# Second-layer products in another order, sums of their weights made later, late gated groups paced by product steps

## The chip, the cores and the metric

The kernel runs on one core of a Trainium2 chip. The metric is the device time of one execution in microseconds (us). Before the change three runs gave 2055.73, 2059.97 and 2067.86 us; the median is 2059.97 us. The profile comes from one further execution of the same program, which took 2061.83 us.

## What is computed

An attention with two parts (downsampled by 4 and put back by repetition, plus a local window of 7 positions) gives x, 2304 tokens of 512 features. A first feed-forward layer with squared relu follows, and then a mixture of eight experts whose gate is balanced over tokens and experts by eight rounds of division:

```python
def _moe2_ref(x, w_gate, w1, w2):
    logits = x @ w_gate                      # 2304 x 8
    P = np.exp(logits - logits.max())
    for _ in range(8):
        P /= P.sum(1, keepdims=True) + 1e-09
        P /= P.sum(0, keepdims=True) + 1e-09
        P *= N / E
    out = np.zeros((N, D), dtype=np.float32)
    for e in range(E):                       # 8 experts
        h = np.maximum(x @ w1[e], 0.0)       # 512 -> 1024
        ye = h @ w2[e]                       # 1024 -> 512
        out += P[:, e:e + 1] * ye
    return out
```

Every expert takes all tokens. The change lies in this mixture, which fills the program from 600 us to the end.

## The kernel before

**Products.** Both layers of an expert are computed as a two-by-two block product with seven block products in place of eight (products 1 to 7). For the second layer a weight block has quarters a[f, d], where f is the parity of the 128-row chunk and d the half of the output columns. Products 1, 2 and 4 take the plain quarters a[0,0], a[1,0] and a[1,1]; products 6, 5, 3 and 7 take sums and differences of quarters (`s2`, `s1`, `s4`, and a[0,0] - a[0,1], which is written over a[0,1]). Each fp32 operand is cut into a high and a low part (`split2`, L462: ScalarE, ACT, writes the high part at L464, VectorE, DVE, or GpSimd, POOL, the difference at L466), and a product of two such operands is three matmuls: high x high, high x low of the input, low of the weight x high.

**First layer.** `l1_second` (L1378) goes through 32 units (8 experts x 4 quarters of the hidden width) times 3 blocks of 768 tokens. `quad` (L1432) combines a unit's products, applies relu and gate on DVE (L1407, L1460), and `store` (L1410) forms sums of the result (L1414, L1416, L1423) and writes them to DRAM as `scr_h`. The first six units finish before the gate rows exist. They are stored without a gate (`scr_c`) and handed to `later` (L1497), which in the middle of the second layer loads such a group back (2 transfers from `scr_c`, 1 of the gate row from `scr_p`), applies the gate with 4 DVE ops (L1520), forms the sums with 4 more (L1525), and writes 6 transfers to `scr_h` (L1528, L1530).

**Second layer.** `l2_second` (L1584) goes through the experts in the order 1 to 7, then 0, and for each through 3 blocks of tokens (`pb`) and the seven products in the order of `PRODUCTS` (L67). One product is 24 matmuls of 128x384 at L1600. Its inputs are two tiles `r` (384 KB each) from `scr_h` (`hidden_loads`, L1564; there are four buffers of this kind), each split by `hidden` (L1577) into a tile named `h`, `i` or `xa`. `collect` (L1614) adds the result to an accumulator; for the first expert it only copies on ACT (L1623), for the others DVE adds (L1627). `l2_weights` (L1540) loads the four quarters of an expert (512 KB each, L1548), makes the four sums (L1556, L1560) and splits all seven weight operands into tiles `w`, `v`, `u`. `finish` (L1631) adds the seven accumulators of a block together (L1638), transposes them on TensorE (PE, L1656) and writes the output.

**What sets the order.** No engine chooses its order on the chip. A planner (class `Order`, L216) runs all these procedures as generators with a cost for each step and writes each engine's instructions in the order that its own clock gives. `("need", f)` holds a procedure back until f is true, `("get", pool)` until a buffer is free, `("wait", event)` until an event fired. Ops that DVE or POOL could do are given to the one that would end first, with `LATE` (3000 ns, L81) in POOL's favour where it is passed (`_w2p`, L369). SyncE (SP) issues every transfer of this part from one in-order queue. `at2["step"]` counts blocks of seven products; the n-th group of `later` is held until that count reaches 1 + 2n.

Of the kernel before, what the change touches and what calls it, by code (L numbers as in the profile page):

```python
# [13 lines left out]
F32R = mybir.dt.float32r  # L14
# [3 lines left out]
ALU = mybir.AluOpType  # L18
# [16 lines left out]
NF2 = DF2 // 128  # L35
# [24 lines left out]
NQ = NF2 // 2  # L60
# [3 lines left out]


OF = {1: (0, 0), 2: (1, 1), 3: (6, 2), 4: (3, 6), 5: (4, 3), 6: (5, 4), 7: (2, 5)}
PRODUCTS = (1, 2, 6, 5, 3, 7, 4)  # L67

BANK = {1: 0, 6: 0, 7: 0, 4: 0, 2: 1, 5: 2, 3: 2}

# [5 lines left out]
NVA, NVD, NQD, NDE, NPT = 1, 2, 2, 2, 2  # L76

AHEAD, WARM, X1FIRST = 3, 4, 3


LATE, SLACK, SLACK_PE = 3000.0, 200.0, 300.0  # L81
# [275 lines left out]
def _dma(nbytes):  # L357
    return ("op", "DMA", nbytes / 360.0)
# [19 lines left out]
def tile_kernel(ctx: ExitStack, tc, qh, kp, vp, qn, kn, vn, vd, bias, mask, w_in, w_out, wg, w12, out):  # L378
# [55 lines left out]
    def get(sl, dt=F32, shape=None, least=1):  # L434
        return ("get", sl, dt, shape, least)
# [734 lines left out]
    PBS = [(0, 0), (1, 0), (0, 1), (0, 2), (1, 1), (1, 2)]  # L1170
    PBS += [(u, pb) for u in range(2, NU - 1) for pb in range(NPB)] + [(NU - 1, 2), (NU - 1, 0), (NU - 1, 1)]
    ev_rows = Event()
    at2 = {"w": 0, "step": -1, "late": 0}
    left_h = {(e, pb): NQ for e in range(E) for pb in range(NPB)}
    s_acc, s_raw, s_h = Many(), Many(), Many()

# [319 lines left out]

    def later(e, pb, q, h):  # L1497

        at2["late"] += 1
        step = min(1 + 2 * at2["late"], 18)  # L1500
        yield ("need", lambda: at2["step"] >= step)
        c = []
        for i in range(3):
            x = yield get(s_p, F32, None, 3 - i)
            c.append(x)
        for i in range(2):
            yield _dma(128 * 2 * TN * 4)
            dma(out=c[i], in_=h[:, 2 * i:2 * i + 2])
        p = c[2]
        a = scr_p[e:e + 1, pb * 2 * TN:(pb + 1) * 2 * TN]  # L1510
        yield _dma(128 * 2 * TN * 4)
        dma(out=p.rearrange("p n t -> p (n t)"),
            in_=bass.AP(tensor=a.tensor, offset=a.offset, ap=[[0, 128], [1, 2 * TN]]))
        t = []
        for i in range(2):
            x = yield get(s_s)
            t.append(x)
        for x, g in ((c[0][:, 0], 0), (c[0][:, 1], 1), (c[1][:, 0], 1), (c[1][:, 1], 0)):
            yield _w2(TN)
            V.scalar_tensor_tensor(out=x, in0=x, scalar=0.0, in1=p[:, g], op0=ALU.max, op1=ALU.mult)  # L1520
        b11, b12, b22, b21 = c[0][:, 0], c[0][:, 1], c[1][:, 0], c[1][:, 1]
        for out, in0, in1, op in ((t[0], b12, b11, ALU.subtract), (t[1], b22, b12, ALU.subtract), (b12, t[1], b11, ALU.add),
                                  (p[:, 0], b21, b12, ALU.subtract)):
            yield _w2(TN)
            V.tensor_tensor(out=out, in0=in0, in1=in1, op=op)  # L1525
        for k, x in ((0, b11), (5, b12), (3, t[0]), (4, t[1]), (6, p[:, 0])):
            yield _dma(128 * TN * 4)
            dma(out=scr_h[e][pb][k, :, q, :], in_=x)  # L1528
        yield _dma(128 * 2 * TN * 4)
        dma(out=scr_h[e][pb][1:3, :, q, :].rearrange("k p t -> p k t"), in_=c[1])  # L1530
        s_p.put(*c)
        s_s.put(*t)
        left_h[e, pb] -= 1
# [5 lines left out]

    def l2_weights():  # L1540
        yield ("need", lambda: at2["w"] == NU)
        for e in EXPERTS:
            a = {}
            for d in range(2):
                for f in range(2):
                    a[f, d] = yield get(s_w)
                    yield _dma(128 * 4096)
                    dma(out=a[f, d], in_=w12[e, f:NF2:2, :, 1, d * 256:(d + 1) * 256].rearrange("q p c -> p q c"))  # L1548
            s1 = yield get(s_w)
            s2 = yield get(s_w)  # L1550
            for k, of in ((1, a[0, 0]), (2, a[1, 0]), (6, s2), (5, s1), (3, None), (7, a[0, 1]), (4, a[1, 1])):
                if k == 1:
                    for out, in0, in1, op in ((s1, a[0, 1], a[1, 1], ALU.add), (a[0, 1], a[0, 0], a[0, 1], ALU.subtract),
                                              (s2, s1, a[0, 0], ALU.subtract)):
                        eng = ENG[(yield _w2p(NQ * 256, LATE))]
                        eng.tensor_tensor(out=out, in0=in0, in1=in1, op=op)  # L1556
                if k == 2:
                    s4 = yield get(s_w)
                    eng = ENG[(yield _w2p(NQ * 256, LATE))]
                    eng.tensor_tensor(out=s4, in0=a[1, 0], in1=s2, op=ALU.subtract)  # L1560
                w2[e, k] = yield from parted(s4 if k == 3 else of, NQ * 256, LATE)
                order.fire(ev_w2[e, k])

    def hidden_loads():  # L1564

# [18 lines left out]
    def l2_second():  # L1584
        for e in EXPERTS:
            for pb in range(NPB):
                at2["step"] += 1
                for k in PRODUCTS:
                    yield ("wait", ev_w2[e, k])
                    w, ps = w2[e, k], []  # L1590
                    for i in range(2):
                        yield ("wait", ev_hk[e, pb, k][i])
                        h = hk.pop((e, pb, k, i))
                        for q in range(2 * i, 2 * i + 2):
                            for d in range(2):
                                if q == 0:
                                    ps.append((yield get(b_q)))
                                yield _pe_r(TN)
                                for m, (a, b) in enumerate(((0, 0), (0, 1), (1, 0))):
                                    PE.matmul(ps[d][:, 0:TN], lhsT=w[a][:, q, d * 128:d * 128 + 128], rhs=h[:, b, q % 2],  # L1600
                                              start=(q == 0 and m == 0), stop=(q == NQ - 1 and m == 2))
                                if q == NQ - 1:
                                    order.add(collect(e, pb, k, d, ps[d]), 1.2)
                        s_h.put(h)
                    if pb == NPB - 1:
                        s_w.put(*w2.pop((e, k)))
                if e == EXPERTS[-1]:
                    order.add(finish(pb), 1.5)
# [22 lines left out]
    def finish(pb):  # L1631

        p = {k: of_acc(pb, k) for k in PRODUCTS}
        yield ("wait", *ev_acc[EXPERTS[-1], pb, 1], *ev_acc[EXPERTS[-1], pb, 2], *ev_acc[EXPERTS[-1], pb, 6])

        def add(out, in0, in1):
            eng = ENG[(yield _w2p(2 * TN))]
            eng.tensor_tensor(out=p[out], in0=p[in0], in1=p[in1], op=ALU.add)  # L1638

        yield from add(2, 1, 2)  # L1640
        yield from add(6, 1, 6)
        yield ("wait", *ev_acc[EXPERTS[-1], pb, 5], *ev_acc[EXPERTS[-1], pb, 3])
        yield from add(1, 6, 5)
        yield from add(3, 1, 3)
        yield ("wait", *ev_acc[EXPERTS[-1], pb, 7], *ev_acc[EXPERTS[-1], pb, 4])
        yield from add(7, 6, 7)
        yield from add(4, 7, 4)
        yield from add(5, 7, 5)
        for nh, (top, low) in enumerate(((2, 4), (3, 5))):
            o = yield get(s_h, F32, [128, 3, 512])  # L1650
            for t in range(3):
# [140 lines left out]
```

## Time and profile before

| | |
|---|---|
| median of three runs | 2059.97 us (2055.73 to 2067.86) |
| the profiled execution | 2061.83 us |
| its span, first to last instruction | 2060.0 us, 30753 instructions |
| mean granted TensorE clock | 0.981 |
| PE busy | 1968.4 us (96%) |
| DVE busy | 1558.6 us (76%) |
| ACT busy | 891.1 us (43%) |
| POOL busy | 671.5 us (33%) |
| transfers | 446.84 MB, mean 217 GB/s |

Busy times are shares of the whole span; stages with different limits are averaged in them. Times within the span are in us from its start. A view of busy time by stages gives for each engine the busy time and in brackets the number of instructions; a timeline gives the start, the length, the engine, the line, what is written and read, and in square brackets how long the engine was idle before and what ended that.

### The profile page before, as it was taken

How to read it: one execution, taken by the hardware profiler on the slowest of the kernel's cores; microseconds unless marked ns; L12 is line 12 of the kernel's file. 1: busy time of each engine (PE TensorE's matmuls, PEld its weight loads, DVE VectorE, ACT ScalarE, POOL GpSimd, SP SyncE). 2: the span in 40 equal slices, each digit the busy share in tenths (PEclk: the TensorE clock that was granted, in tenths of full speed). 3: DMA queues.
4: the chain of work that ended last, by engine and by line, in shares of the span. 5: the costliest groups of instructions: out<-in, count | busy, mean ns of one | idle time of the engine just before them, and what ended most of it. 6: DMA issues, size and time to landing. Idle time of an engine off the chain costs nothing.

```text
span 2060.0 us, 30753 instructions
## 1 busy us (share of the span) xinstructions
PE 1968.4 (96%) x11195; PEld 1854.9 (90%) x11201; DVE 1558.6 (76%) x2140; ACT 891.1 (43%) x1601; POOL 671.5 (33%) x433
## 2 busy tenths in 40 slices
PE   8899998999979999999999999899999989999997
PEld 5577776899979999999999999799999889999997
DVE  6998988681265777777777777667889789988895
ACT  4575546556633222222222222564444344545453
POOL 4445031002004333333333333423424433524451
PEclk8999999999999999999999999899999999999999
DMA  7767686566475666666666667677687768677664
GB/s 200 220 219 226 206 198 196 153 218 210 143 248 194 234 229 212 241 220 228 226 228 235 223 223 264 217 212 236 203 273 233 229 210 283 189 236 229 195 195 143
DMA packets 244848, 446.84 MB, mean 217 GB/s; under 512 B 22440, under 2 KB 144856, under 8 KB 244696
## 3 DMA queue, kind: packets, MB, share of 16 engines
q1 hardware_dynamic: 244696, 444.87, 66.6%
q8 instruction: 88, 1.44, 0.3%
q14 instruction: 64, 0.52, 0.1%
HBM read 280.61 MB, written 164.18 MB: 216 GB/s over the span
## 4 chain that ended last, share of the span: by engine, by line
PE 70%; DVE 14%; DMA 7%; issue 3%; ACT 2%; POOL 1%; SPq 1%; ACTq 0%; DVEq 0%; POOLq 0%
PE b L1374 33%; PE b L1600 23%; PE b L990 6%; PE b L1031 5%; DMA r<-scr_h 3%; DVE xa L466 2%; DMA lk<-in_kp_dram 1%; DVE f L920 1%; DVE f L922 1%; DVE lp L849 1%; DVE z L1525 1%; DVE lp L796 1%; DMA gp<-scr_p 1%; DVE gp L1520 1%; DVE g L1009 1%
## 5 line engine op out<-in xcount | busy, mean ns | idle before, releaser
L1374 PE MATMUL b<-x,w 128*128 128x384 f32 x2688 | 498.0, 338 | 10.3 <-DMA x<-scr_x 4.9
L1374 PEld LDWEIGHTS b<-x,w 128*128 128x128 f32 x2688 | 469.7, 189 | 12.2 <-issue 5.7
L1600 PE MATMUL b<-xa,w 128*128 128x384 f32 x1516 | 342.1, 340 | 13.4 <-DVE xa L466 13.4
L466 DVE TENSOR_TENSOR xa<-r,xa 128x768 fp32r<-128x768 f32 x207 | 285.0, 1387 | 71.1 <-ACT xa L464 68.2
L464 ACT ACTIVATE xa<-r 128x768 fp32r<-128x768 f32 x224 | 189.4, 846 | 238.2 <-DMA r<-scr_h 153.1
L1600 PEld LDWEIGHTS b<-xa,w 128*128 128x128 f32 x1516 | 273.1, 190 | 16.8 <-DVE xa L466 16.7
L1374 PE MATMUL b<-xa,w 128*128 128x384 f32 x1344 | 262.2, 337 | 4.3 <-DMA xa<-scr_x 4.2
L1374 PEld LDWEIGHTS b<-xa,w 128*128 128x128 f32 x1344 | 236.9, 189 | 5.9 <-DMA xa<-scr_x 3.0
L466 POOL TENSOR_TENSOR w<-w,w 128x1024 fp32r<-128x1024 f32 x68 | 151.4, 2227 | 187.1 <-ACT w L464 186.9
L1441 ACT ACTIVATE b<-b 128x384 f32<-128x384 f32 x96 | 45.6, 475 | 326.9 <-PE b L1374 325.3
L1031 PE MATMUL b<-g,s 128*128 128x512 f32 (+1 forms) x756 | 168.9, 369 | 0.9 <-ACT t L1056 0.9
L1447 ACT ACTIVATE q<-b 128x384 f32<-128x384 f32 x192 | 93.3, 490 | 175.6 <-PE b L1374 144.8
L1600 PE MATMUL b<-xa,v 128*128 128x384 f32 x608 | 158.8, 344 | 4.0 <-POOL v L466 2.1
L1228 POOL TENSOR_TENSOR w<-w 128x256 f32<-128x256 f32 x64 | 55.0, 859 | 308.7 <-PE b L1374 257.5
L1031 PEld LDWEIGHTS b<-g,s 128*128 128x128 f32 x756 | 135.9, 188 | 17.9 <-ACT t L1056 1.5
L990 PE MATMUL b<-x,s 128*128 128x512 f32 (+1 forms) x600 | 139.3, 375 | 6.5 <-DVE g L1009 4.8
L1407 DVE SCALAR_TENSOR_TENSOR q<-q,gp 128x768 f32<-128x768 f32 x90 | 127.1, 1412 | 3.1
L990 PEld LDWEIGHTS b<-x,s 128*128 128x128 f32 x600 | 108.0, 191 | 21.8 <-DVE g L1009 6.1
L1471 DVE TENSOR_TENSOR q<-b,q 128x384 f32<-128x384 f32 x96 | 53.5, 557 | 97.8 <-PE b L1374 97.7
L1600 PE MATMUL b<-xa,u 128*128 128x384 f32 x564 | 126.3, 337 | 0.8 <-DVE xa L466 0.6
L1460 DVE SCALAR_TENSOR_TENSOR q<-b,gp 128x384 f32<-128x384 f32 x180 | 100.0, 556 | 34.8 <-PE b L1374 30.7
L1600 PEld LDWEIGHTS b<-xa,v 128*128 128x128 f32 x608 | 113.1, 194 | 5.9 <-POOL v L466 2.4
(250 smaller groups left out, 3337.1 us busy)
## 6 DMA issues: line engine op xcount, KB each, us to landing
r<-scr_h SPq DMA_DIRECT2D x336, 384.0 KB
scr_h<-q SPq DMA_DIRECT2D x90, 576.0 KB
scr_h<-q SPq DMA_DIRECT2D x180, 192.0 KB
scr_h<-q SPq DMA_DIRECT2D x90, 384.0 KB
s<-scr_w SPq DMA_DIRECT2D x85, 256.0 KB
w<-in_w_dram SPq DMA_DIRECT2D x64, 256.0 KB
gp<-scr_p SPq DMA_DIRECT2D x30, 384.0 KB
m<-scr_w SPq DMA_DIRECT2D x43, 256.0 KB
```

Of the source, the lines that this page charges most:

```text
L464: A.activation(out=hi, in_=x, func=AF.Copy)
L466: eng.tensor_tensor(out=lo_, in0=x, in1=hi.bitcast(F32), op=ALU.subtract)
L990: PE.matmul(ps[:, 0:n], lhsT=w[:, a, c], rhs=x[:, b, 0:n], start=(cc == 0 and i == 0), stop=(cc == 3 and i == 2))
L1031: PE.matmul(acc[dc][:, 0:n], lhsT=w[:, a, c], rhs=g[:, b, 0:n], start=(fc == 0 and i == 0), stop=(fc == NF - 1 and i == 2))
L1228: eng.tensor_tensor(out=out, in0=in0, in1=in1, op=op)
L1374: PE.matmul(bank[:, 0:TN], lhsT=w[a][:, iw % 4, cc * 128:cc * 128 + 128], rhs=x[:, b, cc], start=(first and cc == 0 and i == 0), stop=(cc ...
L1407: V.scalar_tensor_tensor(out=x, in0=x, scalar=0.0, in1=p.unsqueeze(1).to_broadcast([128, 2, TN]), op0=ALU.max, op1=ALU.mult)
L1441: A.activation(out=ps[1][:, 0:TN], in_=ps[0][:, 0:TN], func=AF.Copy)
L1447: A.activation(out=c[:, place], in_=ps[bank][:, 0:TN], func=AF.Copy)
L1460: V.scalar_tensor_tensor(out=c[:, i], in0=ps[bank][:, 0:TN], scalar=0.0, in1=p[:, 0], op0=ALU.max, op1=ALU.mult)
L1471: V.tensor_tensor(out=c[:, 2], in0=ps[0][:, 0:TN], in1=c[:, 2], op=ALU.add)
L1600: PE.matmul(ps[d][:, 0:TN], lhsT=w[a][:, q, d * 128:d * 128 + 128], rhs=h[:, b, q % 2], start=(q == 0 and m == 0), stop=(q == NQ - 1 and m ...
```

## The change

Four things are altered. The order of the second layer's products becomes 1, 2, 4, 6, 5, 3, 7, so that the three with plain quarters come first. `l2_weights` splits those three quarters first and makes the sums behind them; for the first expert it passes 0 in place of `LATE`. `at2["step"]` counts products, not blocks; a group of `later` begins at the seventh product, and each of its nine transfers waits for one further product step (`pace`). `finish` adds in an order that fits the new last product.

```diff
-PRODUCTS = (1, 2, 6, 5, 3, 7, 4)
+PRODUCTS = (1, 2, 4, 6, 5, 3, 7)
...
+PACE = 1
...
-    at2 = {"w": 0, "step": -1, "late": 0}
+    at2 = {"w": 0, "step": 0}
...
     def later(e, pb, q, h):
-        at2["late"] += 1
-        step = min(1 + 2 * at2["late"], 18)
-        yield ("need", lambda: at2["step"] >= step)
+        yield ("need", lambda: at2["step"] >= 7)
+
+        def pace():
+            n = at2["step"] + PACE
+            return ("need", lambda: at2["step"] >= n)
+
...
         for i in range(2):
+            yield pace()
             yield _dma(128 * 2 * TN * 4)
             dma(out=c[i], in_=h[:, 2 * i:2 * i + 2])
...
+        yield pace()
         yield _dma(128 * 2 * TN * 4)
...
         for k, x in ((0, b11), (5, b12), (3, t[0]), (4, t[1]), (6, p[:, 0])):
+            yield pace()
             yield _dma(128 * TN * 4)
...
+        yield pace()
         yield _dma(128 * 2 * TN * 4)
...
     def l2_weights():
...
+        late = lambda e: 0.0 if e == EXPERTS[0] else LATE
+
+        def parts(e, k, x):
+            hi = yield get(s_w, F32R)
+            lo_ = yield get(s_w, F32R)
+            yield from split2(x, NQ * 256, hi, lo_, late(e))
+            w2[e, k] = (hi, lo_)
+            order.fire(ev_w2[e, k])
+
         for e in EXPERTS:
             a = {}
-            for d in range(2):
-                for f in range(2):
...
+            for d, f in ((0, 0), (0, 1), (1, 1), (1, 0)):
...
+            for k, of in ((1, a[0, 0]), (2, a[1, 0]), (4, a[1, 1])):
+                yield from parts(e, k, of)
             s1 = yield get(s_w)
             s2 = yield get(s_w)
...
+            for out, in0, in1, op in ((s1, a[0, 1], a[1, 1], ALU.add), (s2, s1, a[0, 0], ALU.subtract)):
+                eng = ENG[(yield _w2p(NQ * 256, late(e)))]
+                eng.tensor_tensor(out=out, in0=in0, in1=in1, op=op)
+            s_w.put(a[1, 1])
+            yield from parts(e, 6, s2)
+            yield from parts(e, 5, s1)
+            s_w.put(s1)
+            for out, in0, in1 in ((s2, a[1, 0], s2), (a[0, 1], a[0, 0], a[0, 1])):
+                eng = ENG[(yield _w2p(NQ * 256, late(e)))]
+                eng.tensor_tensor(out=out, in0=in0, in1=in1, op=ALU.subtract)
+            s_w.put(a[0, 0], a[1, 0])
+            for k, of in ((3, s2), (7, a[0, 1])):
+                yield from parts(e, k, of)
+                s_w.put(of)
...
             for pb in range(NPB):
-                at2["step"] += 1
                 for k in PRODUCTS:
+                    at2["step"] += 1
...
     def finish(pb):
...
+        yield from add(2, 1, 2, 1, 2)
+        yield from add(6, 1, 6, 4, 6)
+        yield from add(4, 6, 4)
+        yield from add(1, 6, 5, 5)
+        yield from add(3, 1, 3, 3)
+        yield from add(5, 1, 7, 7)
+        yield from add(4, 4, 7)
```

What the planner makes of it. Up to the last products of the first layer the instructions are the same in both programs (line numbers move by two). Three places differ in ways that the prediction speaks of.

POOL, from its last op for the first layer on (L466 and L468 with 128x1024 are low parts of weights, L1556, L1560 and L1575 their sums), before:

```order
L466 TENSOR_TENSOR w_1700_12088<-w_1691_12024,w_1699_12087 128x768
L1556 TENSOR_TENSOR w_1720_12277<-w_1717_12251,w_1719_12266 128x1024
L1556 TENSOR_TENSOR w_1717_12251<-w_1705_12126,w_1717_12251 128x1024
L1556 TENSOR_TENSOR v_1722_12299<-w_1720_12277,w_1705_12126 128x1024
L466 TENSOR_TENSOR v_1736_12386<-w_1705_12126,v_1735_12385 128x1024
L1560 TENSOR_TENSOR v_1743_12427<-w_1712_12225,v_1722_12299 128x1024
L466 TENSOR_TENSOR v_1750_12448<-w_1712_12225,v_1749_12447 128x1024
```

and now:

```order
L468 TENSOR_TENSOR w_1700_12088<-w_1691_12024,w_1699_12087 128x768
L468 TENSOR_TENSOR w_1865_13064<-v_1794_12676,w_1829_12846 128x1024
L468 TENSOR_TENSOR v_1872_13105<-w_1801_12695,v_1870_13096 128x1024
L468 TENSOR_TENSOR v_1881_13149<-w_1805_12720,v_1878_13139 128x1024
L1575 TENSOR_TENSOR v_1890_13189<-u_1813_12766,w_1805_12720 128x1024
```

The eleven ops for the first expert are gone from POOL; what now follows is for the second one. They stand on DVE, between the last ops of the first layer (names `q`) and the splits of the second layer's inputs (`h`, `xa`, `i`, read from tiles `r`). DVE there, before:

```order
L1460 SCALAR_TENSOR_TENSOR q_1725_12315<-b_1723_12300,gp_1642_11540 128x384
L1407 SCALAR_TENSOR_TENSOR q_1725_12315<-q_1725_12315,gp_1642_11540 128x768
L466 TENSOR_TENSOR h_1727_12333<-r_1721_12298,h_1727_12333 128x768
L1414 TENSOR_TENSOR q_1737_12405<-q_1725_12315 128x768
L466 TENSOR_TENSOR xa_1732_12369<-r_1728_12334,xa_1732_12369 128x768
L1416 TENSOR_TENSOR q_1737_12405<-q_1737_12405,q_1725_12315 128x384
L1423 TENSOR_TENSOR q_1729_12340<-q_1715_12241,q_1729_12340 128x384
L466 TENSOR_TENSOR xa_1733_12370<-r_1730_12345,xa_1733_12370 128x768
```

and now, up to the low part of the second product's weights (`v_1731`):

```order
L1473 TENSOR_TENSOR q_1725_12315<-b_1723_12300,q_1725_12315 128x384
L468 TENSOR_TENSOR xa_1735_12374<-r_1732_12348,xa_1735_12374 128x768
L1409 SCALAR_TENSOR_TENSOR q_1725_12315<-q_1725_12315,gp_1642_11540 128x768
L1462 SCALAR_TENSOR_TENSOR q_1725_12315<-b_1723_12300,gp_1642_11540 128x384
L1425 TENSOR_TENSOR q_1727_12330<-q_1715_12241,q_1727_12330 128x384
L1416 TENSOR_TENSOR q_1742_12425<-q_1725_12315 128x768
L468 TENSOR_TENSOR xa_1736_12375<-r_1733_12359,xa_1736_12375 128x768
L1418 TENSOR_TENSOR q_1742_12425<-q_1742_12425,q_1725_12315 128x384
L468 TENSOR_TENSOR xa_1740_12412<-r_1737_12387,xa_1740_12412 128x768
L468 TENSOR_TENSOR i_1743_12427<-r_1741_12413,i_1743_12427 128x768
L468 TENSOR_TENSOR h_1745_12437<-r_1744_12428,h_1745_12437 128x768
L468 TENSOR_TENSOR v_1731_12343<-w_1712_12225,v_1730_12342 128x1024
```

The low part of the first product's weights stands ten places ahead of this piece; that of the second stands behind the splits of `r_1737`, `r_1741` and `r_1744`, the fifth to seventh tiles.

SP's queue at the stores of the first late group (`scr_h_0_143`), before:

```order
L1574 DMA r_1944_13489<-scr_h_1_150 128x768
L1528 DMA scr_h_0_143<-gp_1905_13287 128x384 x2
L1528 DMA scr_h_0_143<-z_1913_13315 128x384
L1528 DMA scr_h_0_143<-z_1914_13316 128x384
L1528 DMA scr_h_0_143<-gp_1907_13289 128x384
L1530 DMA scr_h_0_143<-gp_1906_13288 128x2x384
L1574 DMA r_1949_13526<-scr_h_1_150 128x768
```

and now:

```order
L1536 DMA scr_h_0_143<-gp_1796_12689 128x384
L1598 DMA r_1843_12940<-scr_h_2_148 128x768
L1598 DMA r_1848_12966<-scr_h_2_148 128x768
L1536 DMA scr_h_0_143<-gp_1796_12689 128x384
L1598 DMA r_1850_12980<-scr_h_2_148 128x768
L1598 DMA r_1855_13006<-scr_h_2_148 128x768
L1536 DMA scr_h_0_143<-z_1825_12825 128x384
```

Two loads of `r` now stand between any two stores of a group, and the group stands in the first expert.

## Rows read from the trace of the kernel before

**Rows 1.** The page, busy time of each engine (us, share of the span, instructions).

```profile
PE 1968.4 (96%) x11195; PEld 1854.9 (90%) x11201; DVE 1558.6 (76%) x2140; ACT 891.1 (43%) x1601; POOL 671.5 (33%) x433
```

**Rows 2.** Chain of waits in order of time (start, length, what).

```profile
626.58 657.35 PE b L1374 x3786
...
1297.16 3.10 DMA r<-scr_h
...
1303.63 6.23 DMA r<-scr_h
```

**Rows 3.** Busy time by stages: length, PE, PEld, DVE, ACT, POOL, clock, DMA share, GB/s.

```profile
1283.00:1336.00 53.00, 41.30 (x193) 38.95 (x192) 37.67 (x32) 27.97 (x39) 25.32 (x11) 0.81 0.70 229
1336.00:1745.00 409.00, 390.40 (x2184) 383.82 (x2183) 330.24 (x364) 190.24 (x238) 153.65 (x61) 0.98 0.73 235
...
1336.00:1390.00 54.00, 54.00 (x313) 54.00 (x312) 31.78 (x26) 33.94 (x54) 13.30 (x5) 1.00 0.72 215
1390.00:1425.00 35.00, 32.08 (x183) 31.43 (x183) 28.53 (x33) 17.23 (x22) 15.36 (x6) 1.00 0.60 194
...
1465.00:1495.00 30.00, 26.55 (x129) 25.54 (x128) 25.97 (x30) 10.79 (x13) 10.69 (x4) 0.83 0.58 185
1495.00:1530.00 35.00, 33.04 (x187) 32.08 (x187) 28.36 (x33) 17.96 (x22) 13.79 (x6) 1.00 0.73 228
1530.00:1560.00 30.00, 30.00 (x174) 30.00 (x173) 23.58 (x32) 10.71 (x13) 5.23 (x2) 1.00 0.88 306
...
1590.00:1625.00 35.00, 31.30 (x171) 29.25 (x170) 30.36 (x37) 13.62 (x16) 11.72 (x6) 1.00 0.66 214
...
1660.00:1682.00 22.00, 16.80 (x86) 16.16 (x85) 21.89 (x26) 8.68 (x10) 8.12 (x3) 0.92 0.48 134
...
1720.00:1745.00 25.00, 24.29 (x138) 23.59 (x137) 22.66 (x26) 10.17 (x12) 11.53 (x5) 1.00 0.93 316
```

**Rows 4.** PE's timeline: start of the second layer, and 1523 us.

```profile
1290.51 2.29 PE L1374 MATMUL b<-x,w 128*128 128x384 f32 x6 [4.51 <-DVE q L1471]
...
1297.18 3.89 PE L1600 MATMUL b<-h,v 128*128 128x384 f32 x11 [4.06 <-DVE h L466]
...
1522.69 2.01 PE L1600 MATMUL b<-h,w 128*128 128x384 f32 x10 [1.27 <-POOL w L466]
```

**Rows 5.** DVE's and POOL's timeline, 1268 to 1300 us.

```profile
1280.38 0.96 DVE L1407 SCALAR_TENSOR_TENSOR q<-q,gp 128x768 f32<-128x768 f32 x1
...
1286.04 2.67 POOL L1556 TENSOR_TENSOR v<-w,w 128x1024 f32<-128x1024 f32 x1
1286.43 3.10 DVE L1414 TENSOR_TENSOR q<-q 128x768 f32<-128x768 f32 x1
```

**Rows 6.** Instructions of single lines, 1250 to 2060 us (duration min/median/max in ns).

```profile
L466 DVE TENSOR_TENSOR xa<-r,xa x207: 937/958/3171, 1297.9 to 2032.6; 128x768 fp32r<-128x768 f32 x104
...
L464 ACT ACTIVATE xa<-r x224: 827/847/856, 1285.9 to 2031.7; 128x768 fp32r<-128x768 f32 x112
...
L1520 DVE SCALAR_TENSOR_TENSOR gp<-gp,gp x24: 541/551/2685, 1399.2 to 1723.8; 128x384 f32<-128x384 f32 x24
```

**Rows 7.** Timeline within the second late group, 1466 to 1490 us.

```profile
1475.74 2.49 DVE L1520 SCALAR_TENSOR_TENSOR gp<-gp,gp 128x384 f32<-128x384 f32 x1
...
1478.15 3.11 DVE L466 TENSOR_TENSOR xa<-r,xa 128x768 fp32r<-128x768 f32 x1
...
1481.32 4.21 PE L1600 MATMUL b<-xa,w 128*128 128x384 f32 x12 [2.75 <-DVE xa L466]
```

**Rows 8.** Busy time by stages, for the transfers (last two columns).

```profile
1400.00:1750.00 350.00, 331.40 (x1845) 324.82 (x1844) 297.69 (x339) 150.03 (x177) 134.37 (x55) 0.98 0.73 236
1525.00:1550.00 25.00, 25.00 (x146) 25.00 (x145) 21.02 (x29) 10.09 (x13) 5.23 (x2) 1.00 0.90 318
```

**Rows 9.** Timeline of the end.

```profile
2047.27 3.69 DVE L1638 TENSOR_TENSOR q<-q,q 128x768 f32<-128x768 f32 x4
2050.14 4.46 PE L1656 MATMUL b<-ident,q 128*128 128x128 f32 x22 [4.28 <-DVE q L1638]
```

More of the change, by code (lines that the diff above doesn't have):

```diff
@@ L1541, in l2_weights @@
         yield ("need", lambda: at2["w"] == NU)
+        late = lambda e: 0.0 if e == EXPERTS[0] else LATE
[5 more added lines that the diff above has]
+            order.fire(ev_w2[e, k])
         for e in EXPERTS:
             a = {}
-            for d in range(2):
-                for f in range(2):
-                    a[f, d] = yield get(s_w)
-                    yield _dma(128 * 4096)
-                    dma(out=a[f, d], in_=w12[e, f:NF2:2, :, 1, d * 256:(d + 1) * 256].rearrange("q p c -> p q c"))
+            for d, f in ((0, 0), (0, 1), (1, 1), (1, 0)):
+                a[f, d] = yield get(s_w)
+                yield _dma(128 * 4096)
+                dma(out=a[f, d], in_=w12[e, f:NF2:2, :, 1, d * 256:(d + 1) * 256].rearrange("q p c -> p q c"))
+            for k, of in ((1, a[0, 0]), (2, a[1, 0]), (4, a[1, 1])):
+                yield from parts(e, k, of)
@@ L1549, in l2_weights @@
             s1 = yield get(s_w)
             s2 = yield get(s_w)
[L1551 to L1562, printed above, removed]
+            for out, in0, in1, op in ((s1, a[0, 1], a[1, 1], ALU.add), (s2, s1, a[0, 0], ALU.subtract)):
+                eng = ENG[(yield _w2p(NQ * 256, late(e)))]
+                eng.tensor_tensor(out=out, in0=in0, in1=in1, op=op)
@@ L1633, in finish, with add @@
         p = {k: of_acc(pb, k) for k in PRODUCTS}
-        yield ("wait", *ev_acc[EXPERTS[-1], pb, 1], *ev_acc[EXPERTS[-1], pb, 2], *ev_acc[EXPERTS[-1], pb, 6])
-        def add(out, in0, in1):
+        def add(out, in0, in1, *after):
+            for k in after:
+                yield ("wait", *ev_acc[EXPERTS[-1], pb, k])
             eng = ENG[(yield _w2p(2 * TN))]
             eng.tensor_tensor(out=p[out], in0=p[in0], in1=p[in1], op=ALU.add)
[L1640 to L1648, printed above, removed]
+        yield from add(2, 1, 2, 1, 2)
[5 more added lines that the diff above has]
+        yield from add(4, 4, 7)
         for nh, (top, low) in enumerate(((2, 4), (3, 5))):
```

## The prediction

> **What bounds the kernel now.** Begin with the page. TensorE (PE) is busy 96% of the span at a mean clock of 0.98 [rows 1, 3], so only its idle time, and its time at the lower clock, can be won back. The chain of waits gives the full rate: 3786 matmuls in 657.35 us are 0.1736 us each [rows 2], so a second-layer product of 24 takes 4.17 us. Next, busy time by stages, where the losses lie: multiply a stretch's matmuls by 0.1736 and compare with its length. From 1283 to 1336 us the first layer ends and the first seven second-layer products run. The 193 matmuls need 33.5 of 53 us: **19.5 us lost**. From 1336 to 1745 us, 2184 need 379.1 of 409 us: **29.9 us lost** [rows 3]. The change touches both places; 49.4 us is all it can win there.
>
> Why is PE waiting? In the first place, PE's timeline names DVE at the two long gaps [rows 4]. DVE's and POOL's timelines show the cause: a DVE op of 768 columns took 0.96 us at 1280; beside POOL, which makes sums of weights (2.67 us each), the next such op took 3.10 [rows 5]. The usual time is 0.95 [rows 6]. In the second place it is the same pair. The six groups of `later` (8 small DVE ops each) are gated between 1399 and 1724 us [rows 6]. The stretches around them lose 35 - 31.8 = 3.2, 30 - 22.4 = 7.6, 0, 5.3, 7.1 and 1.0 us [rows 3]. The group without loss ran beside next to no POOL work; its ops took 0.55 us. Where POOL splits weights, DVE ops take 2.5 to 3.1 us, PE waits up to 2.75 us [rows 7] and then runs partly at the lower of its two levels, 1.2 GHz (granted clock 0.83 in that stretch) [rows 3].
>
> **Part 1, the first expert's weights.** The order of instructions shows eleven POOL ops (4 sums, 7 low parts) gone to DVE, and nothing left on POOL there. Removed: POOL's 11 ops of some 2.67 us. Added to DVE: 11 ops of 1024 columns. No row shows one on DVE alone; 0.55 us for 384 columns and 0.95 for 768 [rows 6] give 1.2 by the same slope, an estimate, 13.2 us in all. It isn't free: all of it lies ahead of the first seven products.
>
> I follow DVE's order down from 1280.4 us [rows 5], up to where both programs are alike, with these three durations. The low part of product 1's weights is done at 1282.6, the first half of its inputs at 1286.7 (PE waits 0.7 us), the sum on which the last first-layer product waits at 1288.6 (1290.5 before [rows 4]), the second input half at 1288.1. PE does product 1 and that last piece by 1291.9. Then a new wait: product 2's low part `v_1731` stands on DVE behind three splits of tiles whose buffers only come free when the splits ahead of them end, at 1286.7, 1288.1 and 1289.6. A load then needs 3.1 to 6.2 us [rows 2], ACT 0.85 and DVE 0.95 [rows 6], so `v_1731` ends near 1298.2. PE waits 6.3 us; its remaining 22 matmuls of product 2 run, as after the 4.06 us gap [rows 4], at half rate, 0.35 us each, until 1305.9. What stands behind on DVE (two sums 1303, low part of product 6 at 1306) is earlier than PE needs it. Five more products at 4.17 end at 1326.8. Before, the seventh ended at 1336.0 (193 matmuls less 24 of the first layer [rows 3] are seven products): **-9.2 us**. Bounds: loads of 6.2 us and another product at half rate, +5, give -4; no wait at `v_1731` gives -9.2 - 6.3 - 3.8 = -19, all that is lost there.
>
> **Part 2, order of products and sums later.** For later experts products 1, 2, 4 need no sums; POOL's eleven ops per expert are the same. Before, low parts on POOL came late near 1520 us [rows 4], in a stretch that loses 35 - 32.5 = 2.5 us [rows 3]. With three products (12.5 us) ahead of the first sum these waits go: -2.5, counted in part 3's sum. If POOL falls behind instead, product 6 of the second expert is late next. Its high part stands 3.5 products ahead on ACT, 14.6 us, and only a low part of 2.7 us follows it, so I cost that at nothing.
>
> **Part 3, paced groups.** Bytes and ops stay, nine transfers per group, 2.56 MB. They now stand on SP's queue one per product step, two or three loads apart, not in bursts of three and six. A store waiting on its DVE op would hold up the loads behind it; the ops come earlier than the paced stores, so that wait costs nothing. What counts is where the groups meet POOL. By the place of collected products on DVE the groups now lie at products 20, 21 to 24, 33 to 36, 45 to 48, 58 to 62 and 72 to 75 (before 22 to 25, 36, 50, 64, 78, 92). Weights are made around products 18 to 28, 39 to 48, 60 to 69. So the first group lies in the first expert, where DVE is busy 31.78 of 54 us [rows 3], and costs nothing; the third and sixth meet no weights and cost 0.5 us each (0 and 1.0 before); the second, fourth and fifth meet them. Four such groups lost 3.2, 7.6, 5.3 and 7.1, a mean of 5.8; three make 17.4, and the sum is 18.4 against 29.9: **-11.5 us**, weights' waits included. Bounds: all clear, -29.9, or five collisions, 29 us, next to no gain.
>
> **Tail.** The last seven additions run on DVE after the last product, 0.95 us each, and the last transposes wait for them [rows 9]. Before, the first half of the output needed six of them, now all seven: **+0.9 us**.
>
> **Sum.** The profiled execution took 2061.83 us (span 2060.0), 1.86 above the median of the runs. 2061.83 - 9.2 - 11.5 + 0.9 = 2042.0: **2042 us**. Its own range is 2034 to 2051.
>
> **Rivals.**
> A. *Both places come clear*: loads land in 3.1 us, so `v_1731` isn't waited for, and only one group meets POOL. 2061.8 - 18 - 20 + 1 = 2025. For it: the third group before lost nothing. Against: DVE's order puts the splits ahead of `v_1731`. Chance 0.17.
> B. *The pacing only moves the collisions* (or its steps, counted by the planner, don't hold on the chip): the groups lose 28 to 30 us as before and only part 1 counts, 2061.8 - 9.2 + 0.9 = 2053.5; with part 1 at its bad bound, 2058.7. For it: the same eight ops and the same POOL work in the same 400 us. Chance 0.26.
> C. *Slower, transfers become the bound.* From step 8 to 75 a product needs two loads (0.79 MB), 0.10 MB of weights and up to 0.26 MB of a group, 1.15 MB. At full rate that is 276 GB/s; from 1400 to 1750 us the queue moved 236 [rows 8]. Should that be its sustained most, a step takes 4.87 us, 0.70 more, over 67 steps 47 us. With the collisions hidden behind that it gives 47 - 29.9 - 9.2 + 0.9 = +9, with none hidden 18 more; between the two, 2080. It decides once the sustained rate stays under some 242 GB/s. Against it: 318 GB/s over 25 us without a wait of PE [rows 8]. The Trainium skill, DMA: Bandwidth & Descriptors, section "Specifications", puts a core's share of HBM at about 358 GB/s; by it this case would cost nothing, and no run here shows that rate held for long. Chance 0.07.
>
> **Chances and range.** The forecast has 0.50. A measurement can tell about 0.5% from no change, 10.3 us, so faster means below 2051.5 on this scale: forecast and A, with a little of B, **0.69**; same, the rest of B and the forecast's upper edge, **0.23**; slower, C and a part 1 gone wrong, **0.08**. For 8 in 10 the range reaches from A's 2025 to B's 2058.
>
> **What would show it.** Part 1: no POOL op from 1281 to about 1350 us, DVE splits at 0.95 us throughout, one PE gap of some 6 us ahead of the third matmul of product 2, released by a DVE op of 1024 columns, and product 7 done near 1327. Part 3: no burst of three group loads on SP; PE gaps near products 21 to 24, 46 and 60, with DVE ops of 2.5 us beside POOL ops, and none near 34 and 74. PE gaps released by a load of `r` would speak for C, gaps at all six groups for B. The forecast is wrong if the stretch up to product 7 isn't 5 us shorter, or if the stretch behind it still loses over 25 us.

## The result, and the profile after

The changed kernel takes **2043.55 us** (median of four runs, 2043.14 to 2044.38) against 2060.71 us of the kernel before (four runs beside them, 2055.73 to 2067.86). The ratio is 0.9915, with a 95% interval of 0.9885 to 0.9944: faster by 0.85%. The profiled execution took 2043.14 us with a span of 2041.4 us; TensorE's mean granted clock was 0.983.

The page, busy time of each engine after (us, share of the span, instructions), the answer to [rows 1]:

```profile
PE 1964.4 (96%) x11201; PEld 1853.8 (91%) x11201; DVE 1542.9 (76%) x2157; ACT 891.6 (44%) x1601; POOL 626.2 (31%) x416
```

POOL is busy 45 us less and has 17 instructions fewer, DVE has 17 more; yet DVE is busy 16 us less, because its operations are stretched less. PE is busy only 4 us less (time at half clock counts as busy), so most of the gain is idle time.

Busy time by stages after (length, PE, PEld, DVE, ACT, POOL, clock, DMA share, GB/s), the answer to [rows 3]:

```profile
1280.00:1322.00 42.00, 36.27 (x192) 35.67 (x191) 35.63 (x42) 26.03 (x38) 0.00 (x0) 0.92 0.84 288
1322.00:1745.00 423.00, 406.46 (x2293) 401.76 (x2292) 334.36 (x391) 203.27 (x252) 146.22 (x57) 0.99 0.75 238
...
1322.00:1390.00 68.00, 68.00 (x393) 68.00 (x392) 46.51 (x47) 43.17 (x66) 15.69 (x6) 1.00 0.80 254
1390.00:1420.00 30.00, 24.92 (x128) 23.30 (x127) 25.63 (x27) 11.41 (x15) 14.59 (x5) 0.94 0.70 221
1420.00:1485.00 65.00, 65.00 (x375) 65.00 (x374) 54.67 (x69) 31.76 (x37) 21.88 (x9) 1.00 0.82 256
1485.00:1510.00 25.00, 20.83 (x117) 19.87 (x116) 21.28 (x25) 7.69 (x10) 9.12 (x4) 1.00 0.59 182
1510.00:1550.00 40.00, 40.00 (x231) 39.81 (x230) 27.66 (x40) 18.89 (x23) 4.23 (x2) 1.00 0.92 296
1550.00:1580.00 30.00, 25.24 (x134) 24.24 (x133) 27.43 (x29) 10.48 (x12) 14.57 (x6) 0.94 0.44 128
1580.00:1610.00 30.00, 27.48 (x154) 26.54 (x153) 23.17 (x27) 13.63 (x16) 12.81 (x5) 1.00 0.73 249
1610.00:1640.00 30.00, 30.00 (x174) 30.00 (x173) 23.06 (x34) 13.99 (x17) 8.23 (x4) 1.00 0.88 295
1640.00:1745.00 105.00, 105.00 (x603) 105.00 (x602) 84.95 (x100) 52.25 (x61) 45.09 (x18) 1.00 0.71 223
```

With 0.1736 us per matmul again, 1322 to 1745 us loses 423 - 398.1 = **24.9 us**; before, the stretch behind product 7 lost 29.9 [rows 3]. It is lost in four places: 7.8 us from 1390, 4.7 from 1485, 6.7 from 1550 and 3.3 from 1580. The gating operations of the six groups start at 1335, 1381, 1442, 1493, 1551 and 1619 us, so these places are the second, the fourth and the fifth group with what follows it. The four add up to 22.5 us: a matmul on the border of two stretches is counted in both. The first, third and sixth group cost nothing.

The first layer's end and the second layer's start after, timelines of DVE, PE and POOL (start, length, engine, line, what, idle time before it and what ended that), the answer to [rows 4, 5]:

```profile
1285.75 0.95 DVE L1409 SCALAR_TENSOR_TENSOR q<-q,gp 128x768 f32<-128x768 f32 x1
...
1291.30 0.96 DVE L468 TENSOR_TENSOR i<-r,i 128x768 fp32r<-128x768 f32 x1 [0.21 <-ACT i L466]
1292.18 0.95 DVE L468 TENSOR_TENSOR h<-r,h 128x768 fp32r<-128x768 f32 x1
1293.05 1.22 DVE L468 TENSOR_TENSOR v<-w,v 128x1024 fp32r<-128x1024 f32 x1
...
1294.32 8.98 PE L1624 MATMUL b<-xa,v 128*128 128x384 f32 x34 [5.73 <-DVE v L468]
...
1357.75 2.39 POOL L468 TENSOR_TENSOR w<-v,w 128x1024 fp32r<-128x1024 f32 x1 [100.87 <-DVE i L468]
```

POOL does nothing for 100 us. No DVE operation is stretched: 768 columns take 0.95 us, 1024 columns 1.22. The gap of 4.51 us ahead of the first layer's last piece and that of 4.06 us in product 1 [rows 4] are gone. One of 5.73 us stands in product 2 in their place, on the low part that waited behind the input splits; the 34 matmuls behind it take 8.98 us, 3.1 more than at the full rate.

**Where the time went, measured from one operation.** Up to a 768-column gating operation on DVE (L1407 before, L1409 after; two more of its kind follow before the first layer ends) the two programs are the same. It starts at 1273.08 us before and at 1269.86 after: 3.2 of the 18.7 us between the profiled executions lie ahead of anything that the change touches. So the table counts from there, to the end of product 7 (the 168th second-layer matmul; each trace holds all 4032 of them), and from there to the end of the span. Each row is one execution. How much these stretches vary between executions of one kernel was not measured, so differences of a few us rest on a single profile each. "After" is the full change, the others are the experiments below; all are in us.

| kernel | to product 7 | product 7 to end | median of its runs |
|---|---|---|---|
| before | 63.1 | 723.8 | 2060.71 |
| after | 52.2 | 719.3 | 2043.55 |
| weights alone | 50.7 | 726.7 | 2050.79 |
| paced groups alone | 62.2 | 712.4 | 2052.10 |
| old order, weights on DVE | 57.3 | 724.3 | 2057.71 |
| first expert's weights on POOL | 69.3 | 718.3 | 2061.13 |
| groups in POOL-free products | 52.2 | 701.4 | 2025.16 |
| the same in bursts | 51.3 | 699.9 | 2026.44 |
| groups on the weights | 51.1 | 727.3 | 2057.67 |
| product 2's low part first | 52.7 | 716.5 | 2045.02 |
| POOL-free, low part first | 52.5 | 697.0 | 2023.24 |
| the same, tail swapped | 52.8 | 698.2 | 2023.32 |

The full change wins 10.8 us up to product 7 and 4.6 us behind it, 15.4 together; the medians differ by 17.2.

### The profile page after: what moved, and what is told of

The parts are those of the page before. It is cut to its first block, busy times and chain, and to the rows that moved or that the text cites. A ratio compares the mean times of both kernels' runs of the same rounds, so it can differ in the third digit from the quotient of the medians.

```text
span 2041.4 us, 30758 instructions
## 1 busy us (share of the span) xinstructions
PE 1964.4 (96%) x11201; PEld 1853.8 (91%) x11201; DVE 1542.9 (76%) x2157; ACT 891.6 (44%) x1601; POOL 626.2 (31%) x416
## 4 chain that ended last, share of the span: by engine, by line
PE 79%; DVE 9%; DMA 7%; issue 2%; ACT 2%; POOL 1%; SPq 1%; DVEq 0%; ACTq 0%; POOLq 0%
PE b L1376 33%; PE b L1624 31%; PE b L992 6%; PE b L1033 6%; DMA o<-in_w_in_dram 1%; DMA r<-scr_h 1%; DMA lk<-in_kp_dram 1%; DVE f L922 1%; DVE xa L468 1%; DVE f L924 1%; DVE lp L851 1%; DMA x<-scr_x 1%; DMA o<-in_w_out_dram 1%; DMA lk<-in_vp_dram 0%; DMA xa<-scr_x 0%
## 5 line engine op out<-in xcount | busy, mean ns | idle before, releaser
L468 DVE TENSOR_TENSOR xa<-r,xa 128x768 fp32r<-128x768 f32 x210 | 260.3, 1253 | 63.1 <-ACT xa L466 62.4
L466 ACT ACTIVATE xa<-r 128x768 fp32r<-128x768 f32 x224 | 189.5, 846 | 243.5 <-DMA r<-scr_h 136.1
L1624 PE MATMUL b<-xa,w 128*128 128x384 f32 x1232 | 263.4, 337 | 5.4 <-DVE xa L468 5.4
L1376 PE MATMUL b<-xa,w 128*128 128x384 f32 x1344 | 263.7, 339 | 3.0 <-DMA xa<-scr_x 3.0
L1376 PEld LDWEIGHTS b<-xa,w 128*128 128x128 f32 x1344 | 238.5, 190 | 4.6 <-DMA xa<-scr_x 3.7
L1624 PEld LDWEIGHTS b<-xa,w 128*128 128x128 f32 x1232 | 219.6, 189 | 6.8 <-DVE xa L468 6.7
L468 POOL TENSOR_TENSOR w<-w,w 128x1024 fp32r<-128x1024 f32 x71 | 158.6, 2234 | 191.8 <-ACT w L466 191.7
L1624 PE MATMUL b<-xa,u 128*128 128x384 f32 x736 | 186.6, 337 | 3.1 <-DVE xa L468 3.1
L1624 PE MATMUL b<-xa,v 128*128 128x384 f32 x720 | 167.9, 342 | 5.7 <-DVE v L468 5.7
L1624 PEld LDWEIGHTS b<-xa,u 128*128 128x128 f32 x736 | 134.0, 188 | 4.0 <-DVE xa L468 4.0
L1624 PEld LDWEIGHTS b<-xa,v 128*128 128x128 f32 x720 | 131.7, 192 | 6.1 <-DVE v L468 6.1
L1409 DVE SCALAR_TENSOR_TENSOR q<-q,gp 128x768 f32<-128x768 f32 x90 | 125.1, 1390 | 3.1
```

Source lines behind the costliest of these rows:

```text
L466: A.activation(out=hi, in_=x, func=AF.Copy)
L468: eng.tensor_tensor(out=lo_, in0=x, in1=hi.bitcast(F32), op=ALU.subtract)
L1376: PE.matmul(bank[:, 0:TN], lhsT=w[a][:, iw % 4, cc * 128:cc * 128 + 128], rhs=x[:, b, cc], start=(first and cc == 0 and i == 0), stop=(cc ...
L1409: V.scalar_tensor_tensor(out=x, in0=x, scalar=0.0, in1=p.unsqueeze(1).to_broadcast([128, 2, TN]), op0=ALU.max, op1=ALU.mult)
```

## The experiments

The kernel before ran beside every batch; each ratio is to those runs.

### The two halves apart

The full change with the groups of the kernel before:

```diff
-        yield ("need", lambda: at2["step"] >= 7)
...
-            yield pace()
...
+        at2["late"] += 1
+        step = 7 * min(1 + 2 * at2["late"], 18) + 1
+        yield ("need", lambda: at2["step"] >= step)
```

> The change without its paced groups: groups start at the old blocks (products 22, 36, 50, ...) and issue their transfers in bursts. My theory: the transition up to product 7 keeps its whole gain of about 10.8 us, the groups cost what they did before (about 25 us, with only the 2.5 us of weights' waits gone): 2060.7 - 10.8 - 2.5 = about 2047 us, 4 us above the full change. Rival: the early products need the paced groups too, or the weights' new order makes the groups worse; then 2052 us or more.

Measured: 2050.79 us, ratio 0.9945 (0.9924 to 0.9966). That is between my theory (2047) and the rival (2052 or more). The transition keeps its gain (50.7 us), and the rest is no better than before (726.7 against 723.8). The waits on late weights near 1520 us [rows 4] are gone, but the 2.5 us that I had counted for them don't appear: of the 48 small group operations (4 gating, 4 sums in each group) 17 take over 1 us there, 13 before.

The kernel before with the new `later` and the count of products:

```diff
-                at2["step"] += 1
                 for k in PRODUCTS:
+                    at2["step"] += 1
...
-        step = min(1 + 2 * at2["late"], 18)
-        yield ("need", lambda: at2["step"] >= step)
+        yield ("need", lambda: at2["step"] >= 7)
...
+            yield pace()
```

> The kernel before with paced, back-to-back groups only; sums and products of the second layer in their old order, the first expert's on VectorE and GpSimd as before. My theory: the 19.5 us of the transition stay lost, the groups lose some 5 us less than their 29.9: about 2056 us. Rival B of the prediction (pacing only moves the collisions): 2061 us, no change. A third reading, that the gain behind product 7 came from the weights' order and not from the pacing, also gives 2061 here, and then the run with the weights alone gives the full change's 2043.

Measured: 2052.10 us, ratio 0.9942 (0.9923 to 0.9960). The transition is as it was (62.2), and behind product 7 11.4 us are gone. That is more than I expected, and more than the full change wins there (4.6). In these profiles, then, the halves don't add. By the medians that is not clear of noise: the halves win 0.55 and 0.58%, the full change 0.85%, each known to 0.2 or 0.3. It isn't that more of the full change's groups meet POOL: 11 of the 48 operations take over 1 us in the full change, 14 in the run with paced groups alone. But in the full change PE also waits 2.9 us for late weights (shown below), and between product 7 and 1745 us the granted clock falls to its lower level twice (from 1413 and from 1567 us), in the other run never. Why a collision costs more there wasn't tried. Third reading refuted: pacing alone does gain.

### Does the place of a group decide?

The full change, with each group tied to a product number. By its timeline POOL makes weights near products 16 to 27, 37 to 52, 58 to 73 and so on, every 21. A group's DVE operations come some four to seven products behind its start, so one that starts at 8 + 21n has them ahead of that work, and one that starts at 17 + 21n within it:

```diff
-        yield ("need", lambda: at2["step"] >= 7)
+        at2["late"] += 1
+        first = 8 + 21 * at2["late"]
+        yield ("need", lambda: at2["step"] >= first)
```

(`late` starts at -1; the second kernel has 17 in place of 8.)

> The full change, but each group starts at a product in which GpSimd makes no weights: groups start at products 8, 29, 50, 71, 92 and 113 instead of back to back; the pacing of one transfer per product stays. My theory (a group costs where its small VectorE operations meet GpSimd's weight work, 0.5 us elsewhere): of the 24.9 us lost behind product 7 about 18 go, 2043.5 - 18 = about 2026 us. Rival (what is lost there is the transfers, or GpSimd against the splits of inputs with no group in it): within 4 us of 2043.5, whatever the place.

> The full change, but all six groups start four products before a new expert begins (products 17, 38, 59, 80, 101, 122), so that their VectorE operations fall into GpSimd's weight work each time. My theory: six collisions at 5.8 us each, 35 us against the 24.9 lost now: 2043.5 + 10 = about 2053 us. Rival (place doesn't matter): 2043.5 within 3 us.

Measured: 2025.16 us, ratio 0.9817 (0.9790 to 0.9844), and 2057.67 us, ratio 0.9983 (0.9960 to 1.0007). My theory held for the first (2026) and was 5 us low for the second (2053). Same work, same pacing, the same number of transfers: 32.5 us between the two, and only the place of the groups differs. The transfers move with the operations, but no PE gap over 0.3 us behind product 7 is ended by a load in either run. The gating operations' durations point at the operations (minimum, median and maximum in ns, first and last start). After:

```profile
L1527 DVE SCALAR_TENSOR_TENSOR gp<-gp,gp x24: 544/551/2769, 1335.0 to 1624.8; 128x384 f32<-128x384 f32 x24
```

In the POOL-free products, with the busy time by stages:

```profile
L1529 DVE SCALAR_TENSOR_TENSOR gp<-gp,gp x24: 546/550/560, 1340.7 to 1792.5; 128x384 f32<-128x384 f32 x24
...
1324.00:1745.00 421.00, 419.12 (x2395) 417.09 (x2394) 349.08 (x401) 211.81 (x262) 151.83 (x58) 1.00 0.76 239
```

On the weights, with the timelines of DVE and PE:

```profile
L1529 DVE SCALAR_TENSOR_TENSOR gp<-gp,gp x24: 540/548/2605, 1390.9 to 1872.2; 128x384 f32<-128x384 f32 x24
...
1679.29 2.53 DVE L1529 SCALAR_TENSOR_TENSOR gp<-gp,gp 128x384 f32<-128x384 f32 x1
1681.74 3.15 DVE L468 TENSOR_TENSOR i<-r,i 128x768 fp32r<-128x768 f32 x1
...
1699.20 0.44 PE L1626 MATMUL b<-xa,u 128*128 128x384 f32 x1 [2.52 <-DVE xa L468]
```

Away from POOL no gating operation exceeds 0.56 us, and the stretch, which holds five of the six groups, loses 421 - 415.8 = 5.2 us in place of 24.9. POOL is as busy there as in the full change (151.83 us), and it stretches even more of the input splits: from product 8 to product 134, 69 of the 242 on DVE take over 1.3 us, against 52 of 239 in the full change and 30 of 247 in the kernel with its groups on the weights. So stretching alone costs little; it costs where a group's operations stand on DVE beside it. On the weights, operations of 2.5 and splits of 3.15 us make PE wait at every group, at the first one also 4.28 and 1.42 us for late weights.

The POOL-free kernel with its transfers in bursts (`PACE = 0`):

> Groups start at products 8, 29, 50, 71, 92 and 113 as in the run with placed groups, but issue their transfers in bursts as the kernel before does. My theory (place alone decides): within 3 us of 2025. Rival (a burst of 1.2 MB ahead of the input loads makes TensorE wait some 1 us at each of the six groups): 2030 us or more, with TensorE gaps released by loads.

Measured: 2026.44 us, ratio 0.9826 (0.9800 to 0.9852); my theory held, and no PE gap over 0.6 us behind product 7 is ended by a load. The pacing wins nothing that can be measured once the place is right: what it did in the change was to move the groups. Five of the groups here have one operation of 1.5 us beside POOL, at no cost that shows. In bursts some splits of inputs move to POOL and its weights come late instead (PE's timeline):

```profile
1759.95 2.00 PE L1626 MATMUL b<-xa,v 128*128 128x384 f32 x10 [0.80 <-POOL v L468]
1765.52 2.03 PE L1626 MATMUL b<-h,w 128*128 128x384 f32 x10 [1.14 <-POOL w L468]
```

### What wins in the transition?

The full change with the first expert's weights on POOL where it is free:

```diff
-        late = lambda e: 0.0 if e == EXPERTS[0] else LATE
+        late = lambda e: LATE
```

> The full change, but the first expert's sums and low parts go to GpSimd wherever it is free, as the later experts' do; the order of products (1, 2, 4 first) stays. My theory (the gain of the transition is VectorE freed of the work beside it): input splits of some 3 us come back, a gap of 3 to 5 us ahead of the last piece of the first layer, and 7 to 10 us of the gain are lost: about 2052 us. Rival (the gain is the product order, which needs no sums at the start): within 3 us of 2043.5.

Measured: 2061.13 us, ratio 0.9988 (0.9973 to 1.0002): not 2052, the whole gain is gone. Up to product 7 it takes 69.3 us, 6.2 more than the kernel before. Timelines of POOL, DVE and PE:

```profile
1291.59 2.59 POOL L468 TENSOR_TENSOR v<-w,v 128x1024 fp32r<-128x1024 f32 x1 [1.36 <-ACT v L466]
1291.90 3.09 DVE L468 TENSOR_TENSOR h<-r,h 128x768 fp32r<-128x768 f32 x1
...
1295.04 0.69 PE L1624 MATMUL b<-h,w 128*128 128x384 f32 x1 [5.10 <-DVE h L468]
...
1319.06 1.01 PE L1624 MATMUL b<-h,u 128*128 128x384 f32 x2 [7.41 <-ACT u L466]
```

The gap of 5.10 us was expected; that of 7.41 us at product 6, whose sum is now made late and is then split on ACT, was not. Making sums later, with POOL still making them, is a loss here up to product 7.

The kernel before with the first expert's weights on DVE, in the old order:

```diff
+        late = lambda e: 0.0 if e == EXPERTS[0] else LATE
...
-                        eng = ENG[(yield _w2p(NQ * 256, LATE))]
+                        eng = ENG[(yield _w2p(NQ * 256, late(e)))]
...
-                w2[e, k] = yield from parted(s4 if k == 3 else of, NQ * 256, LATE)
+                w2[e, k] = yield from parted(s4 if k == 3 else of, NQ * 256, late(e))
```

> The kernel before (old product order, old groups), with only the first expert's sums and low parts taken from GpSimd to VectorE. Three sums then stand ahead of product 1's low part on VectorE, and that part behind six input splits. My theory (both halves are needed: no op beside VectorE and no sums ahead of the first product): the operations keep 0.95 us but a gap of some 6 to 10 us opens ahead of product 1's low part, and the stretch up to product 7 is as long as before, 2061 us within 5. Rival (VectorE freed of GpSimd is the whole gain): 2050 us, as the run with the weights alone.

Measured: 2057.71 us, ratio 0.9969 (0.9952 to 0.9985). Between the theories: 57.3 us up to product 7, 5.7 less than before and 5.1 more than after. PE's and DVE's timelines:

```profile
1295.65 1.01 PE L1601 MATMUL b<-h,v 128*128 128x384 f32 x2 [5.32 <-ACT v L464]
...
1297.72 1.22 DVE L466 TENSOR_TENSOR v<-w,v 128x1024 fp32r<-128x1024 f32 x1
...
1299.00 3.41 PE L1601 MATMUL b<-h,v 128*128 128x384 f32 x10 [2.33 <-DVE v L466]
```

The operations are short, but product 1 waits 5.32 + 2.33 us for its weights behind the sums and splits. So DVE in POOL's place wins about half, and the three products without sums the other half, but only with it. Whether the first half comes from splits that are no longer stretched or from DVE's shorter operations (1.22 us against 2.67 on POOL [rows 5]) these runs don't tell apart.

### Can the 5.73 us gap be won?

The full change with the later input splits held back:

```diff
     def hidden(e, pb, k, i, r):
+        if e == EXPERTS[0] and pb == 0 and k in PRODUCTS[2:]:
+            yield ("wait", ev_w2[e, 2])
```

> The full change, but the splits of the first block's inputs from the third product on stand behind product 2's low part on VectorE, so that this part no longer waits for three loads. My theory: the 5.73 us gap ahead of product 2 and the 3.4 us at half clock behind it both go, and at most 1 us appears at product 4: about 8 us less, 2035 us. Rival (the gap is only moved: the loads of product 4's inputs, or its low part, are the next late thing): under 2 us less, 2042 us.

Measured: 2045.02 us, ratio 0.9906 (0.9883 to 0.9929); 52.7 us up to product 7 against 52.2. My theory fell. PE's timeline:

```profile
1300.99 4.11 PE L1626 MATMUL b<-xa,v 128*128 128x384 f32 x22 [2.61 <-DVE v L468]
...
1306.92 2.00 PE L1626 MATMUL b<-i,v 128*128 128x384 f32 x10 [0.65 <-DVE v L468]
...
1313.38 0.85 PE L1626 MATMUL b<-h,u 128*128 128x384 f32 x2 [2.37 <-ACT u L466]
```

The gap halves, and its rest comes back at products 4 and 6. DVE is busy 35.63 of the 42 us of this stretch after (first row of the stages): that its total of work, not its order, holds PE there fits both, but wasn't tried by itself.

### The faster version

POOL-free groups and the low part first:

> Groups in the products without weight work, and product 2's low part ahead of the later input splits. My theory: both gains add, since one lies ahead of product 7 and the other behind it: 2025 - 8 = about 2017 us. Rival: the gap is moved behind product 2 and only the placing counts, 2024 us.

Measured: 2023.24 us, ratio 0.9806 (0.9782 to 0.9830). The rival held: the placing counts, the low part adds nothing that can be told. Then with the last two additions swapped:

```diff
-        yield from add(5, 1, 7, 7)
-        yield from add(4, 4, 7)
+        yield from add(4, 4, 7, 7)
+        yield from add(5, 1, 7)
```

> Placed groups, product 2's low part first, and the last two additions swapped, so that the first half of the output waits for six additions again, not seven. My theory of the tail: the last wait of TensorE falls from 5.02 us to some 4.1 (one addition of 0.95), and the time from 2023.2 to about 2022 us, which the timing alone cannot tell. Rival (the last copy out of the accumulators, not the additions, holds it): the wait stays 5.0.

Measured: 2023.32 us, ratio 0.9800 (0.9775 to 0.9824). PE's last wait after, the answer to [rows 9]:

```profile
2031.60 3.93 PE L1679 MATMUL b<-ident,q 128*128 128x128 f32 x22 [5.02 <-DVE q L1663]
```

And in this kernel:

```profile
2009.71 4.58 PE L1683 MATMUL b<-ident,q 128*128 128x128 f32 x22 [4.15 <-DVE q L1667]
```

The row shows the addition's 0.87 us; the timing can't. By their ratios these versions are 2% faster than the kernel before and 1% faster than the change.

## Why the prediction was right, and which step was not

2042 us was forecast and 2043.55 measured, inside the range of 2025 to 2058 and the forecast's own 2034 to 2051; faster had 0.69. That the total is so close is partly luck: by the count from the common operation the change wins 15.4 us where the sum had 19.8, and 3.2 us of the profiled difference lie ahead of the change.

**Part 1, -9.2 us forecast, -10.8 measured: right, by its steps.** The 1024-column operation takes 1.22 us (estimate 1.2), POOL is idle, no split is stretched. The new wait came at the named tile, behind the named splits: 5.73 us (6.3 forecast). The half-rate matmuls cost 3.1 us more than at full rate (3.8 forecast). Product 7 was done at 1322.1 us, 1325.3 on the scale of the profile before, against 1326.8. The 0.7 us wait for the first inputs of product 1 did not come.

**Part 2, -2.5 us and no late weights: wrong.** With the weights alone no gain shows behind product 7. And weights are late again, at the second group, though not those of product 6, which I had named. Timelines of POOL, DVE, ACT and PE after:

```profile
1380.51 2.40 POOL L468 TENSOR_TENSOR w<-u,u 128x1024 fp32r<-128x1024 f32 x1 [5.86 <-ACT u L466]
...
1392.84 0.51 PE L1624 MATMUL b<-h,u 128*128 128x384 f32 x2
...
1394.94 3.15 DVE L468 TENSOR_TENSOR xa<-r,xa 128x768 fp32r<-128x768 f32 x1
1397.24 3.12 POOL L1582 TENSOR_TENSOR u<-v,u 128x1024 f32<-128x1024 f32 x1
1398.02 1.01 DVE L1651 TENSOR_TENSOR y<-b,y 128x384 f32<-128x384 f32 x2
1398.15 0.44 PE L1624 MATMUL b<-xa,u 128*128 128x384 f32 x1 [0.76 <-DVE xa L468]
...
1408.57 1.04 ACT L466 ACTIVATE w<-u 128x1024 fp32r<-128x1024 f32 x1
1409.66 0.62 PE L1624 MATMUL b<-h,w 128*128 128x384 f32 x2 [1.10 <-ACT w L466]
1409.69 2.36 POOL L468 TENSOR_TENSOR w<-u,w 128x1024 fp32r<-128x1024 f32 x1 [6.26 <-ACT w L466]
1412.11 2.75 PE L1624 MATMUL b<-h,w 128*128 128x384 f32 x10 [1.82 <-POOL w L468]
```

Product 6 of the second expert (from 1392.84) does not wait: its low part was done at 1382.9, so costing it at nothing was right. PE first waits on stretched splits, then, at product 7, 1.10 us for the high part of its weights and 1.82 for the low part. The step that failed is "With three products (12.5 us) ahead of the first sum these waits go": before, the late weights near 1520 us were those of products 7 and 4, the last two of the old order, so what was late is the end of an expert's eleven operations and not the first sum, and product 7 now stands at that end. Its sum was ready at 1400.4; ACT's queue held the high part until 1408.57, behind input splits that waited for DVE and for a load.

**Part 3, -11.5 us forecast: the term that was mis-sized.** The groups that cost something were named rightly (second, fourth and fifth), and so was the mechanism: the placed groups show it. Their places were right but for the first (products 10 to 12, not 20). That the third and sixth "meet no weights" was not quite so: one sum of the third took 2.76 us and two operations of the sixth 1.3, at no cost, as one of 1.83 us in the third group before, of which I wrote 0.55. But "three make 17.4" gave three the mean of four old ones. They cost 7.8, 4.7 and 6.7 + 3.3 us, 22.5 in all: the second has the weights' waits of Part 2, the fifth a gap of 3.33 us, half-rate matmuls and 30 us of catching up. With the tail, 4.6 us are won behind product 7. That the paced groups alone win 11.4 us there with more stretched operations speaks against a sum by the number of collisions; what decides between 4.7 and 10 us was only read from the trace, not tried.

**Tail, +0.9 forecast, +0.74 measured** (5.02 against 4.28 us [rows 9]), and taken back by the swap.

**Rivals.** A's 2025 us was reached, but by placing the groups and with the wait at `v_1731` still there; in the change itself neither place came clear. B was half right: pacing is worth only the places to which it moves the groups. C is out: the transfers ran at 296 GB/s for 40 us and at 254 for 68 us with full PE rate, above the 242 at which it would have decided, and no gap behind product 7 over 0.6 us is ended by a load. The figure of 358 GB/s that the prediction sets beside C (the Trainium skill, DMA: Bandwidth & Descriptors, section "Specifications") was neither reached nor contradicted.

The Trainium skill, SBUF — State Buffer, section "Who interferes with whom", says that a VectorE operation with two inputs in SBUF contends with a GpSimd operation that reads SBUF, and one with at most one SBUF input, outside the two-port modes, does not. The rows above agree: the split of two SBUF tiles takes 3.15 us beside POOL, while L1651, which reads PSUM and SBUF, takes 1.01 for two inside a POOL operation.

## What to carry to other kernels

When two engines slow each other, the question for each piece of movable work is what runs beside it, not how evenly its transfers are spread: tie it to the stretch in which the other engine is idle, and check the longest duration of its operations in the trace. A rule that starts work "as early as possible, one piece after another" leaves that place to chance, and what two changes win apart may then not add. Where one engine makes a series of inputs, look after a change of order at the last of them too, not only at the first. Where a stretch is bound by one engine's total, as the transition seems to be by DVE, a better order only moves the gap.

## What the runs showed of the hardware

- The same instructions ahead of the change took different times: the common gating operation started between 1268.49 and 1286.51 us in twelve profiled executions. Counting from it removes that; single profiles can't be compared by their spans to 10 us.
- POOL is stretched as well as DVE: after the change one of its splits of 1024 columns (L468) took 2.39 us at 1357.75, beside one DVE split of 2.50 us, and one 3.12 at 1400.31, beside two that took 5.30 together.
- After the change, in the stretch from 1485 to 1510 us, with PE gaps of 1.61, 1.16 and 1.39 us, the granted clock stayed at 1.00. In that from 1550, with a gap of 3.33 us, it was 0.94, and in that from 1390, where gaps of 1.10 and 1.82 us stand two matmuls apart, 0.94 too; behind both some matmuls ran at half rate, 0.32 us each.
